# W_out's sums nearer to their loads in three phases, low parts at other places, last halves in tiles of their own

## The chip, the cores and the metric

The kernel runs on one core of one Trainium2 chip. The metric is the device time of one execution in microseconds. The engines are named as in the profile: PE is TensorE, DVE is VectorE, ACT is ScalarE, POOL is GpSimd, SP is SyncE, which here issues nearly all DMAs.

## What is computed

Three stages in a row, all in fp32:

```
# 1. retention: B=2, H=8, S=768, D=64
state = gamma[h] * state + k[:, :, t] (x) v[:, :, t]
y[:, :, t] = scale * q[:, :, t] @ state
# 2. mixture of 8 experts on x [1536, 512], F = 1024
P = exp(x @ w_gate - max); 8 times: P /= rows, P /= columns, P *= N / E
out = sum over e of P[:, e:e+1] * (relu(x @ w1[e]) @ w2[e])
# 3. dense layer, d_ff = 2048
h = x @ w_in;  g = max(h, 0) + alpha * min(h, 0);  y = g @ w_out
```

## The kernel before

**Arithmetic.** An fp32 matmul is done as three fp32r matmuls (mm3, L323 to L325): each operand is split into a high part (a copy rounded to fp32r, made by ACT) and a low part (operand minus high part, made by DVE or POOL), and the products high by high, low by high and high by low are summed in PSUM. So each matrix needs a "high" and a "low" step before PE can use it. Products of 2x2 blocks are done with seven multiplications instead of eight, on sums of the blocks, which are prepared ahead ("sums", "adds").

**Phases.** After the retention part come 20 phases: phase 0 to 7 and 8 to 15 are the eight experts for the two halves of the tokens, 16 to 19 the dense layer as two more "experts" of 1024 columns. Phases 8 to 19 use the seven products for the second layer as well; a phase there has 56 positions: 28 products of the first layer, written (column, product) in the texts, and 28 of the second, written by a number, where the number 1 comes at position 29, 2 at 30 and so on. One position is six matmuls of 128x384 and takes about 1.04 us. While an expert's second phase runs (8 to 15), the kernel also prepares W_out for the dense layer and stores it in DRAM (tensor c).

**Order.** The order is written by hand. `step(ph, pos, fn)` hangs a piece of work behind the PE work of one position; pieces at one position are issued in the order in which they were registered. Each engine carries out its instructions in the order of the program, and so does SP with its DMA issues. What waits, waits with everything behind it on its engine. An entry `[2, ...]` in `unkept` (L302 and others) is issued two positions after the one that appended it.

**What the change touches.** `dense_prep(i)` (L271 and after) prepares one piece of W_out in six steps: `load` (L280, a DMA into the tile dr), `high(0)` (L285, ACT, dw<-dr) whose result is stored two positions later by L310 and L311 (SP), `low(0)` (L289, DVE, into the same tile dw, from dr and dw) stored in the same way, `sums` (L299, four operations of POOL on dr in place), `high(1)`, `low(1)`. Their positions were 6, 14, 24, 27, 40, 52 in each of phases 8 to 15. In a fast phase the hidden layer's blocks b11, b12, b21, b22 come from the first layer's products (copies L977, L997 on ACT, additions L992 on DVE); t1 to t4 (L1059 to L1065, DVE) are their sums, `hhigh` (L1085, ACT) and `hlow` (L1093, DVE) split them into the tiles hs for the second layer. `decode_at` (L882 to L903 on DVE, L892 on ACT) decodes a part of the dense layer's weights between. L179 is the low part of a w1 matrix, L146 its sums, L228 the low part of a w2 matrix, L939 the low part of hidden values in phases 0 to 7. The first loads come from `load_qk` (L471), the last output tiles are written by `last_sum` (L1145 to L1148): one half copied from PSUM by DVE, the other by ACT, each stored by its own DMA queue.

Of the kernel before, what the change touches and what calls it, by code (L numbers as in the profile page):

```python
# [8 lines left out]
F32 = mybir.dt.float32  # L9
# [3 lines left out]
AF = mybir.ActivationFunctionType  # L13
# [10 lines left out]
E, F = 8, 1024  # L24
# [3 lines left out]
HT = S // 2  # L28
# [19 lines left out]
def tile_kernel(ctx, tc, lead, qkT, kv, ctab, w_gate, w1, w2, w_in, w_out, alpha, out):  # L48
    nc = tc.nc
# [392 lines left out]
    with tc.manual_schedule():  # L442

        with ExitStack() as actx:
# [20 lines left out]
            def load_qk(i):  # L465
                if i >= NST:
                    return
                if i == 0:
                    cut = nt + NP * C
                    for cols in (slice(0, cut), slice(cut, lead.shape[1])):  # L470
                        nc.sync.dma_start(out=head[:, cols], in_=lead[:, cols])  # L471
                    halves = head[:, nt:].rearrange("p (v a b c) -> p v a b c", v=2, a=2, c=C)
                    qk_t[i] = lambda r, a, p: halves[r, p // 2, a, p % 2, :]
                else:
                    t = ld.tile([128, 2, NP, C], F32, tag="qk", name=f"qk{i}")
                    nc.sync.dma_start(out=t.rearrange("p a b c -> p (a b c)"), in_=qkT[i])
                    qk_t[i] = lambda r, a, p, t=t: t[r, a, p, :]
# [22 lines left out]
            dve.memset(ones, 1.0)  # L500
            first = tmp.tile([128, HT], F32, tag="d", bufs=2, name="first")
            nc.scalar.activation(out=first[:, 0:1], in_=ones[:, 0:1], func=AF.Copy)
            load_qk(0)
            load_qk(1)
# [636 lines left out]
        def last_sum(ps, m, h):  # L1141
            o = pools["fast"].tile([128, HT], F32, tag=f"t{m}{h}", name=f"last_{m}{h}")
            c = S * (B - 1) + HT * h
            w = HT // 2
            nc.vector.tensor_copy(o[:, 0:w], ps[:, 0:w])  # L1145
            nc.sync.dma_start(out=out[128 * m:128 * m + 128, c:c + w], in_=o[:, 0:w])
            nc.scalar.activation(out=o[:, w:HT], in_=ps[:, w:HT], func=AF.Copy)
            nc.scalar.dma_start(out=out[128 * m:128 * m + 128, c + w:c + HT], in_=o[:, w:HT])  # L1148

# [145 lines left out]
        for ph in range(len(PHASES)):  # L1295
# [41 lines left out]
            else:  # L1337
# [3 lines left out]
                else:  # L1341
# [5 lines left out]
                    for m, part, hi, lo, eng in (  # L1347
                        (2, "a", 5, 5, pool), (2, "c", 9, 9, pool), (2, "b", 11, 12, dve),
                        (3, "a", 13, 16, dve), (3, "c", 14, 14, pool), (3, "b", 17, 17, pool),
                        (4, "a", 25, 26, dve), (4, "c", 30, 31, dve), (4, "b", 37, 37, dve),  # L1350
                        (5, "a", 34, 34, dve), (5, "c", 34, 34, dve), (5, "b", 37, 37, dve),
# [8 lines left out]
                early = ((4, 6, 7, dve), (9, 12, 13, dve), (15, 16, 20, dve), (22, 25, 26, dve))  # L1360
                first = ((6, 6, 7, dve), (12, 13, 14, dve), (20, 20, 20, pool), (24, 24, 24, pool))
                for j, (hi, l0, l1, eng) in enumerate(early if ph else first):
# [5 lines left out]
            if fast:  # L1368
# [7 lines left out]
                if ph < 2 * E:  # L1376
                    step(ph, 0, lambda ph=ph: weight_load(ph))
                    for pos, fn in zip((6, 14, 24, 27, 40, 52), dense_prep(ph - E)):
                        step(ph, pos, fn)
                o = ph < 2 * E  # L1380
                for pos, fn, jp in (
# [3 lines left out]
                    step(ph, pos, lambda ph=ph, fn=fn, jp=jp: fn(ph, jp))  # L1385
                highs = (11, 23, 19, 30 - o, 25, 33 - o, *((32, 34, 36, 38) if o else (33, 34, 37, 39)), 41, 43, 47, 49)
                lows = (13, 26, 20, 31 - o, 27, 34 - o, *((33, 35, 37, 39) if o else (35, 36, 38, 40)), 42, 44, 48, 50)
                for k in range(14):
# [178 lines left out]
```

## Time and profile before

| what | value |
|---|---|
| median of 3 runs | 1256.41 us (1254.65 to 1256.62) |
| the profiled execution's own time | 1257.15 us |
| its span, first to last instruction | 1255.4 us |
| PE busy | 1247.3 us (99%) |
| DVE, ACT, POOL busy | 1010.4, 649.8, 449.0 us |
| mean DMA rate | 299 GB/s |

The busy time of PE is the sum of its matmuls' times, with ends that are modelled; a gap shorter than the overlap of two matmuls does not show in it. The chain of waits follows the last instruction back to what released it, step by step. A row of a timeline gives the start, the busy time, the engine and the line; in brackets stands how long the engine was idle before and what ended that.

### The profile page before, as it was taken

How to read it: one execution, taken by the hardware profiler on the slowest of the kernel's cores; microseconds unless marked ns; L12 is line 12 of the kernel's file. 1: busy time of each engine (PE TensorE's matmuls, PEld its weight loads, DVE VectorE, ACT ScalarE, POOL GpSimd, SP SyncE). 2: the span in 40 equal slices, each digit the busy share in tenths (PEclk: the TensorE clock that was granted, in tenths of full speed). 3: DMA queues.
4: the chain of work that ended last, by engine and by line, in shares of the span. 5: the costliest groups of instructions: out<-in, count | busy, mean ns of one | idle time of the engine just before them, and what ended most of it. 6: DMA issues, size and time to landing. Idle time of an engine off the chain costs nothing.

```text
span 1255.4 us, 20476 instructions
## 1 busy us (share of the span) xinstructions
PE 1247.3 (99%) x7325; PEld 1186.9 (95%) x7325; DVE 1010.4 (80%) x1548; ACT 649.8 (52%) x1204; POOL 449.0 (36%) x407
## 2 busy tenths in 40 slices
PE   9999999999999999999999999999999999999998
PEld 7888989899999989899999999999999999999998
DVE  6676888888888888878596969687877899887867
ACT  5643645453544444446364553545464657656573
POOL 4732343525252625101033333242413464716100
PEclk9999999999999999999999999999999999999999
DMA  9795999999999999899999889898989987694615
GB/s 353 256 275 168 314 339 361 325 354 329 349 327 354 324 352 330 284 348 346 362 308 351 292 320 325 299 349 298 351 303 327 319 281 224 244 314 160 216 37 184
DMA packets 223126, 375.09 MB, mean 299 GB/s; under 512 B 16560, under 2 KB 136752, under 8 KB 223024
## 3 DMA queue, kind: packets, MB, share of 16 engines
q1 hardware_dynamic: 222736, 373.58, 88.0%
q8 instruction: 58, 0.95, 0.3%
q14 instruction: 44, 0.36, 0.1%
q10 hardware_dynamic: 288, 0.20, 0.0%
HBM read 241.04 MB, written 131.11 MB: 296 GB/s over the span
## 4 chain that ended last, share of the span: by engine, by line
PE 87%; DMA 6%; DVE 5%; issue 1%; ACT 0%; SPq 0%; POOL 0%; DVEq 0%; ACTq 0%
PE B L323 7%; PE B L325 7%; PE B L324 7%; PE o L325 7%; PE o L323 7%; PE o L324 7%; PE A L323 6%; PE A L325 6%; PE A L324 6%; PE D L324 4%; PE E L325 4%; PE E L323 4%; PE E L324 4%; PE D L325 4%; PE D L323 4%; DMA dr<-wd 1%
## 5 line engine op out<-in xcount | busy, mean ns | idle before, releaser
L1085 ACT ACTIVATE hs<-b 128x768 fp32r<-128x768 f32 x168 | 139.0, 842 | 66.9 <-DVE b L1059 23.7
L146 POOL TENSOR_TENSOR raw<-raw 128x256 f32<-128x256 f32 x112 | 111.3, 1004 | 69.7 <-DMA raw<-in_w_dram 33.9
L1093 DVE TENSOR_TENSOR hs<-b,hs 128x768 fp32r<-128x768 f32 x120 | 122.4, 1025 | 15.0 <-ACT hs L1085 14.6
L256 POOL TENSOR_TENSOR pr<-pr 128x256 f32<-128x256 f32 x52 | 50.7, 975 | 188.6 <-DMA pr<-in_w_dram 62.2
L323 PE MATMUL A<-xh,W 128*128 128x384 f32 x320 | 107.3, 335 | 0.0
L325 PE MATMUL A<-xh,W 128*128 128x384 f32 x320 | 107.2, 335 | 0.0
L324 PE MATMUL A<-xl,W 128*128 128x384 f32 x320 | 107.0, 334 | 0.0
L323 PE MATMUL B<-hs,ws 128*128 128x384 f32 x288 | 96.4, 335 | 0.2 <-ACT W L169 0.2
L1152 POOL TENSOR_TENSOR total<-total,t 128x384 f32<-128x384 f32 x56 | 73.1, 1333 | 65.4 <-DVE t L1123 65.4
L325 PE MATMUL B<-hs,ws 128*128 128x384 f32 x288 | 96.3, 334 | 0.0
L324 PE MATMUL B<-hs,ws 128*128 128x384 f32 x288 | 96.2, 334 | 0.0
L169 ACT ACTIVATE W<-raw 128x512 fp32r<-128x512 f32 (+1 forms) x126 | 85.9, 695 | 19.3 <-DVE raw L146 19.3
L396 POOL TENSOR_TENSOR xs<-b,xs 128x384 fp32r<-128x384 f32 x19 | 24.6, 1296 | 185.4 <-ACT xs L392 128.5
L323 PE MATMUL B<-xh,W 128*128 128x384 f32 x268 | 90.5, 338 | 0.0
L179 POOL TENSOR_TENSOR W<-raw,W 128x512 fp32r<-128x512 f32 (+1 forms) x48 | 74.5, 1565 | 43.4 <-PE B L325 18.8
L325 PE MATMUL B<-xh,W 128*128 128x384 f32 x268 | 89.7, 335 | 0.0
L324 PE MATMUL B<-xl,W 128*128 128x384 f32 x268 | 89.6, 334 | 0.0
L992 DVE TENSOR_TENSOR b<-E,b 128x384 f32<-128x384 f32 x48 | 26.6, 555 | 74.7 <-ACT W L169 51.9
L977 ACT ACTIVATE B<-A 128x384 f32<-128x384 f32 x48 | 22.8, 476 | 120.6 <-PE A L325 120.4
L299 POOL TENSOR_TENSOR dr<-dr 128x256 f32<-128x256 f32 x32 | 37.9, 1185 | 130.5 <-DVE dw L289 105.5
L323 PE MATMUL D<-xh,W 128*128 128x384 f32 x236 | 79.0, 335 | 0.0
L325 PE MATMUL D<-xh,W 128*128 128x384 f32 x236 | 79.0, 335 | 0.0
(498 smaller groups left out, 4010.2 us busy)
## 6 DMA issues: line engine op xcount, KB each, us to landing
ws<-c SPq DMA_DIRECT2D x168, 512.0 KB, 5.9
raw<-in_w_dram SPq DMA_DIRECT2D x64, 512.0 KB, 5.6
c<-W SPq DMA_DIRECT2D x64, 384.0 KB, 6.5
W<-c SPq DMA_DIRECT2D x22, 768.0 KB, 7.8
pr<-in_w_dram SPq DMA_DIRECT2D x32, 512.0 KB, 5.8
c<-pw SPq DMA_DIRECT2D x32, 512.0 KB, 7.0
c<-pr SPq DMA_DIRECT2D x32, 512.0 KB, 7.6
raws<-in_w_dram SPq DMA_DIRECT2D x32, 384.0 KB, 6.2
```

What stands on the lines that cost most here:

```text
L146: eng.tensor_tensor(out=out, in0=in0, in1=in1, op=op)
L169: nc.scalar.activation(out=hi, in_=src, func=AF.Copy)
L179: eng.tensor_tensor(out=lo, in0=src, in1=hi.bitcast(F32), op=ALU.subtract)
L256: eng.tensor_tensor(out=out, in0=in0, in1=in1, op=op)
L299: nc.gpsimd.tensor_tensor(out=out, in0=in0, in1=in1, op=op)
L323: nc.tensor.matmul(ps, ah, bh, start=first, stop=False, skip_group_check=True)
L324: nc.tensor.matmul(ps, ah, bl, start=False, stop=False, skip_group_check=True)
L325: nc.tensor.matmul(ps, alo, bh, start=False, stop=last, skip_group_check=True)
L992: nc.vector.tensor_tensor(out=dst, in0=src, in1=dst, op=ALU.add)
L1085: nc.scalar.activation(out=t[:, 0, :], in_=hsource(ph, k), func=func)
L1093: nc.vector.tensor_tensor(out=lo, in0=src, in1=hi.bitcast(F32), op=ALU.subtract)
L1152: eng.tensor_tensor(out=dst, in0=dst, in1=tt[m, h], op=ALU.add)
```

## The change

- `load_qk(0)`: the second of the two DMAs that load `head` is issued by ACT instead of SP, and the call stands ahead of ACT's first instruction.
- `last_sum`: the half that ACT copies gets an SBUF tile of its own, under a tag of another buffer.
- Phase 0: the low parts of w1 matrix 3 part a go from position 16 to 14, of matrix 4 part a from 26 to 30 and part c from 31 to 32; the two low parts of w2 matrix 1 go from 13 and 14 to 17 and 18.
- `dense_prep`: in phases 8 and 15 low(0) goes from 24 to 17 and the sums from 27 to 18; in phase 9 high(0) goes from 14 to 18, low(0) from 24 to 21, the sums from 27 to 22. At one position these pieces are registered ahead of t1 and the hhigh and hlow steps.
- Phases 16 to 19: hhigh 0 goes from 11 to 14, hlow 0 from 13 to 16, hlow 4 from 27 to 32.

```diff
--- before.py
+++ after.py
@@ -467,8 +467,8 @@
                     return
                 if i == 0:
                     cut = nt + NP * C
-                    for cols in (slice(0, cut), slice(cut, lead.shape[1])):
-                        nc.sync.dma_start(out=head[:, cols], in_=lead[:, cols])
+                    for cols, eng in ((slice(0, cut), nc.sync), (slice(cut, lead.shape[1]), nc.scalar)):
+                        eng.dma_start(out=head[:, cols], in_=lead[:, cols])
                     halves = head[:, nt:].rearrange("p (v a b c) -> p v a b c", v=2, a=2, c=C)
                     qk_t[i] = lambda r, a, p: halves[r, p // 2, a, p % 2, :]
                 else:
@@ -499,8 +499,8 @@
             warm(WARM)
             dve.memset(ones, 1.0)
             first = tmp.tile([128, HT], F32, tag="d", bufs=2, name="first")
+            load_qk(0)
             nc.scalar.activation(out=first[:, 0:1], in_=ones[:, 0:1], func=AF.Copy)
-            load_qk(0)
             load_qk(1)
             load_kv(0)
             load_kv(1)
@@ -1144,8 +1144,9 @@
             w = HT // 2
             nc.vector.tensor_copy(o[:, 0:w], ps[:, 0:w])
             nc.sync.dma_start(out=out[128 * m:128 * m + 128, c:c + w], in_=o[:, 0:w])
-            nc.scalar.activation(out=o[:, w:HT], in_=ps[:, w:HT], func=AF.Copy)
-            nc.scalar.dma_start(out=out[128 * m:128 * m + 128, c + w:c + HT], in_=o[:, w:HT])
+            o = pools["fast"].tile([128, HT], F32, tag=f"t{m - 2}0", name=f"end_{m}{h}")
+            nc.scalar.activation(out=o[:, 0:w], in_=ps[:, w:HT], func=AF.Copy)
+            nc.scalar.dma_start(out=out[128 * m:128 * m + 128, c + w:c + HT], in_=o[:, 0:w])
 
         def gather(m, h, eng=nc.gpsimd):
             dst = total[:, S * m + HT * h:S * m + HT * h + HT]
@@ -1346,8 +1347,8 @@
                     step(ph, 10, lambda: w1_adds(3, pool))
                     for m, part, hi, lo, eng in (
                         (2, "a", 5, 5, pool), (2, "c", 9, 9, pool), (2, "b", 11, 12, dve),
-                        (3, "a", 13, 16, dve), (3, "c", 14, 14, pool), (3, "b", 17, 17, pool),
-                        (4, "a", 25, 26, dve), (4, "c", 30, 31, dve), (4, "b", 37, 37, dve),
+                        (3, "a", 13, 14, dve), (3, "c", 14, 14, pool), (3, "b", 17, 17, pool),
+                        (4, "a", 25, 30, dve), (4, "c", 30, 32, dve), (4, "b", 37, 37, dve),
                         (5, "a", 34, 34, dve), (5, "c", 34, 34, dve), (5, "b", 37, 37, dve),
                     ):
                         step(ph, hi, lambda m=m, part=part: w1_high(m, part))
@@ -1358,7 +1359,7 @@
                     w1_at(ph, n + 4, dve, dve, 29, 29, 30, 31, 32, 31, 32)
                     w1_at(ph, n + 5, dve, dve, 33, 33, 34, 35, 36, 35, 36)
                 early = ((4, 6, 7, dve), (9, 12, 13, dve), (15, 16, 20, dve), (22, 25, 26, dve))
-                first = ((6, 6, 7, dve), (12, 13, 14, dve), (20, 20, 20, pool), (24, 24, 24, pool))
+                first = ((6, 6, 7, dve), (12, 17, 18, dve), (20, 20, 20, pool), (24, 24, 24, pool))
                 for j, (hi, l0, l1, eng) in enumerate(early if ph else first):
                     step(ph, hi, lambda m=n + j: w2_high(m))
                     step(ph, l0, lambda m=n + j, eng=eng: w2_low(m, 0, eng))
@@ -1375,7 +1376,12 @@
                         step(ph, (2, 5, 8, 11)[q // 2], lambda m=q // 2, h=q % 2: gather(m, h))
                 if ph < 2 * E:
                     step(ph, 0, lambda ph=ph: weight_load(ph))
-                    for pos, fn in zip((6, 14, 24, 27, 40, 52), dense_prep(ph - E)):
+                    places = (6, 14, 24, 27, 40, 52)
+                    if ph in (E, 2 * E - 1):
+                        places = (6, 14, 17, 18, 40, 52)
+                    elif ph == E + 1:
+                        places = (6, 18, 21, 22, 40, 52)
+                    for pos, fn in zip(places, dense_prep(ph - E)):
                         step(ph, pos, fn)
                 o = ph < 2 * E
                 for pos, fn, jp in (
@@ -1383,8 +1389,8 @@
                     (29 - o, t1, 1), (32 - o, t2, 1), (32 if o else 37, t3, 1),
                 ):
                     step(ph, pos, lambda ph=ph, fn=fn, jp=jp: fn(ph, jp))
-                highs = (11, 23, 19, 30 - o, 25, 33 - o, *((32, 34, 36, 38) if o else (33, 34, 37, 39)), 41, 43, 47, 49)
-                lows = (13, 26, 20, 31 - o, 27, 34 - o, *((33, 35, 37, 39) if o else (35, 36, 38, 40)), 42, 44, 48, 50)
+                highs = (11 if o else 14, 23, 19, 30 - o, 25, 33 - o, *((32, 34, 36, 38) if o else (33, 34, 37, 39)), 41, 43, 47, 49)
+                lows = (13 if o else 16, 26, 20, 31 - o, 27 if o else 32, 34 - o, *((33, 35, 37, 39) if o else (35, 36, 38, 40)), 42, 44, 48, 50)
                 for k in range(14):
                     step(ph, highs[k], lambda ph=ph, k=k: hhigh(ph, k))
                     step(ph, lows[k], lambda ph=ph, k=k: hlow(ph, k))
```

## Rows read from the trace of the kernel before

**Rows 1.** Page, part 1: busy us (share of the span) x instructions.

```profile
span 1255.4 us, 20476 instructions
...
PE 1247.3 (99%) x7325; PEld 1186.9 (95%) x7325; DVE 1010.4 (80%) x1548; ACT 649.8 (52%) x1204; POOL 449.0 (36%) x407
```

**Rows 2.** Page, part 4: the chain that ended last, share of the span by engine.

```profile
PE 87%; DMA 6%; DVE 5%; issue 1%; ACT 0%; SPq 0%; POOL 0%; DVEq 0%; ACTq 0%
```

**Rows 3.** Waits of PE, whole span: total us, times, longest.

```profile
PE sc L534 <- DMA qk<-in_qkT_dram: 1.2, 1, 1.2
...
PE E L323 <- ACT E L977: 0.9, 1, 0.9
...
PE o L325 <- DVE hl L939: 0.7, 1, 0.7
```

**Rows 4.** Timeline of DVE, phase 8: start us, us, engine, line, operation [idle before].

```profile
566.37 0.96 DVE L1059 TENSOR_TENSOR b<-b,b 128x768 f32<-128x768 f32 x1 [2.25 <-ACT b L997]
...
569.56 0.69 DVE L887 SCALAR_TENSOR_TENSOR a<-rd,a 128x512 f32<-128x512 uint32 x1
...
574.68 1.23 DVE L289 TENSOR_TENSOR dw<-dr,dw 128x1024 fp32r<-128x1024 f32 x1 [0.77 <-DMA W<-c]
...
577.98 2.43 DVE L1093 TENSOR_TENSOR hs<-b,hs 128x768 fp32r<-128x768 f32 x2
```

**Rows 5.** Tile dw, 547 to 610 us: durations in ns, starts; time to landing.

```profile
L311 SPq DMA_DIRECT2D c<-dw x2: 319/332/346, 567.7 to 577.1; - x2
...
DMA to landing us min/median/max: 6.9/7.7/8.3
```

**Rows 6.** Timeline of ACT, phase 8.

```profile
571.40 0.71 ACT L892 ACTIVATE ex<-ex,ebias 128x512 uint32<-128x512 uint32 x1
...
572.05 0.47 ACT L977 ACTIVATE E<-B 128x384 f32<-128x384 f32 x1
```

**Rows 7.** Timeline of PE, phase 8.

```profile
572.89 0.33 PE L323 MATMUL E<-xh,pairs 128*128 128x384 f32 x1
...
573.95 0.33 PE L323 MATMUL E<-xh,W 128*128 128x384 f32 x1
...
579.23 0.34 PE L323 MATMUL A<-hs,ws 128*128 128x384 f32 x1
```

**Rows 8.** Timeline of ACT, phase 9.

```profile
625.22 1.06 ACT L285 ACTIVATE dw<-dr 128x1024 fp32r<-128x1024 f32 x1 [2.00 <-DMA dr<-wd]
```

**Rows 9.** Timeline of DVE, phase 9.

```profile
630.63 0.69 DVE L887 SCALAR_TENSOR_TENSOR a<-rd,a 128x512 f32<-128x512 uint32 x1
...
638.18 2.44 DVE L1093 TENSOR_TENSOR hs<-b,hs 128x768 fp32r<-128x768 f32 x2
```

**Rows 10.** Tile dw, 620 to 632 us.

```profile
DMA to landing us min/median/max: 4.0/4.0/4.1
```

**Rows 11.** Timeline of DVE, phase 15.

```profile
977.31 0.96 DVE L1059 TENSOR_TENSOR b<-b,b 128x768 f32<-128x768 f32 x1 [2.26 <-ACT b L997]
...
988.17 2.44 DVE L1093 TENSOR_TENSOR hs<-b,hs 128x768 fp32r<-128x768 f32 x2
```

**Rows 12.** Tile dw, 972 to 990 us.

```profile
L310 SPq DMA_DIRECT2D c<-dw x2: 370/370/371, 976.1 to 986.0; - x2
...
DMA to landing us min/median/max: 2.1/4.2/6.3
```

**Rows 13.** Timeline of DVE, phase 0.

```profile
67.79 1.40 DVE L179 TENSOR_TENSOR W<-raw,W 128x512 fp32r<-128x512 f32 x1
```

**Rows 14.** Timelines of DVE in phase 16 and of ACT in phase 17.

```profile
1052.66 0.96 DVE L1093 TENSOR_TENSOR hs<-b,hs 128x768 fp32r<-128x768 f32 x1 [0.91 <-ACT hs L1085]
...
1090.02 0.84 ACT L1085 ACTIVATE hs<-b 128x768 fp32r<-128x768 f32 x1
```

**Rows 15.** Timeline of DVE, start.

```profile
7.45 0.42 DVE L572 TENSOR_TENSOR k<-kt,head 128x256 f32<-128x256 f32 x1 [0.26 <-ACT k L569]
```

**Rows 16.** Windows: us, busy of PE, PEld, DVE, ACT, POOL (x), PEclk, DMA share, GB/s.

```profile
1254.00:1255.40 1.40, 0.00 (x0) 0.00 (x0) 0.00 (x0) 0.00 (x0) 0.00 (x0) 0.65 0.01 2
```

## The prediction

> **What bounds the kernel now.** I began with the busy times and the chain of waits [rows 1, 2]: TensorE is busy 1247.3 of 1255.4 us and holds 87% of the chain that ended last. Nothing that another engine saves shortens this kernel unless TensorE was waiting for it, so I went on to TensorE's own waits [rows 3]. There are few: 1.2 us for the first loads, 0.9 us for a copy of ScalarE, 0.7 us for a low part of VectorE. With short gaps that this view does not list (0.2 to 0.4 us each, read from the starts of neighbouring matmuls, which are 0.173 us apart where nothing waits) some 4.4 us could go, start aside. Everything that makes TensorE wait anew counts in full, because TensorE has no spare time later. So the question for each move is not what it costs its own engine, but whether the work queued behind it still comes before TensorE needs it. I read the engines' timelines around each moved step for that.
>
> The profiled execution took 1257.15 us (1.75 around the span); the median of the runs shown is 1256.41, 0.74 less. I add the change to the median; against the profile the same sum would give 0.74 more. A difference of 0.2%, 2.5 us, is about what a measurement can tell.
>
> **Phase 8, low(0) from position 24 to 17.** This is the term that decides. low(0) overwrites the tile dw, whose high part two DMAs (L310, L311) are still reading, so it waits until both have landed. Its position in the program does not move them: high(0) stays at 14 and the stores are issued two positions later, at 566.5 and 567.7. They take 6.9 us at the least to land [rows 5], in a stretch where the DMA engines are full; landing is at about 574.6, and the row of low(0) shows it: even at position 24 VectorE sat idle 0.77 us before it, and it started at 574.68 [rows 4]. So low(0) at 17 can't start earlier than now, and the sums behind it don't come earlier either. But VectorE takes its work in order, and low(0) now stands ahead of t1 (L1059), which ran at 566.37. All that VectorE did from there to 573.9, 7.3 us of work, goes behind low(0)'s end at 575.9.
>
> Who waits for that: L887 ran at 569.56, three quarters of a microsecond long. After low(0) come t1 (0.96), one L992 (0.47 to the next start), L179, L882, L884 and L887, together 3.2 us, so L887 ends near 579.1. ScalarE's L892 waits for it (0.71, it was at 571.40), and in ScalarE's queue the copy E<-B stands behind that; it was at 572.05 [rows 6] and comes at 579.8 and ends near 580.3. TensorE needs it for the group that began at 573.95 [rows 7]: 6.3 us late. Before it, the group at 572.89 waits for the L992 of 567.96, which now ends at 577.4: 4.5 us without a matmul. Then hlow1 (the first of the two L1093 at 577.98, one half of 2.43 us, so done at 579.2 just as TensorE took it at 579.23) comes behind low(0)'s 575.9 and the 7.3 us, plus the 3.3 us that lay between low(0) and its end now: 586.5, 7.3 us late. From this comes +7.0 us (bounds: 5.7, if the work after the wait packs without the gaps seen now, and 7.9, if POOL's four sums slow the VectorE work beside them as they do now, two L1093 taking 2.43 instead of 1.9 [rows 4]). SP gets stuck as well: the store of low(0)'s result is issued at its new position and waits for 575.9, with three weight loads behind it that went out from 568.2 to 570.9. They go out some 7 us later, but the queue has run empty by 574.6 and TensorE is late by the same 7 us: nothing more for them.
>
> **Phase 9, high(0) 14 to 18, low(0) 24 to 21.** Removed: ScalarE stood 2.00 us in front of high(0) [rows 8], because the load of dr had not landed, and behind it the copy that TensorE lost 0.9 us for [rows 3], with a slower restart 1.1 us. Four positions of 1.04 us cover the 2.0 us. Added: the stores now go out two positions after 18, near 630, and low(0) stands at 21, ahead of t2. VectorE would reach it at 631.3, after L887 [rows 9]. The stores there took 4.0 us [rows 10]; less, if the stall of phase 8 has drained the queue, down to the 2.1 of phase 15 [rows 12]. So VectorE waits to about 633.3, 2 us, and from 630.6 to hlow1's end at 639.2 (half of the row at 638.18) it had no pause to make that up. Net -1.1 - 0.3 (a gap 18 us later) + 2.0 + 0.1: +0.7 us. Bounds: -1.5 (no wait) and +4 (landing 6.9 us after issue as in phase 8).
>
> **Phase 15, low(0) 24 to 17.** The same move, but here the queue is quick: issued at 976.1 and 976.5, 2.1 us at the least [rows 12], landed at 978.7. VectorE is free from 975.05 (2.26 us of idle stand ahead of t1, which ran at 977.31 [rows 11]); t1 now starts at about 980.0 (978.75 + 1.22), 2.7 us late. What catches that up is the 1.22 us that low(0) took later, and a few short idle stretches (0.67, 0.21), at most 1 us of which are usable. hlow1 ended at 989.4 (the first of two at 988.17), TensorE takes it at 990.2. The sums' 5 us go to 980 to 985, and lie beside more of VectorE's two-input work than before, which costs 0.3 to 0.5 for each 128x768 operation. 2.7 - 1.2 - 0.8 + 1.4 = +2.1 us, less a gap of 0.4 late in the phase that goes because w1's sums start earlier: +1.7. Bounds -0.4 (only that gap) and +3.5 (no catching up, full contention).
>
> **Phase 0.** Four low parts move by 1 to 5 positions. The o group waited 0.7 us for hl [rows 3], and a low of 1.40 us held a matmul 0.24 us [rows 13]. Both lose what stood in front of them on VectorE; but the softmax reductions between them wait for a load that landed at 81.0, and this stays. -0.75 us, bounds 0 and -1.2. A raw load that starts after the moved w2 low part goes out 4 us later; it was just in time, so +3 is the far end in the other direction.
>
> **Phases 16 to 19.** hlow4 leaves the queue ahead of t1, so hhigh3 (which made VectorE wait 0.91 us at 1052.66) comes earlier, and hhigh0 (0.84 us on ScalarE) goes from in front of a copy [rows 14]. TensorE's gaps behind them are 0.42 and 0.30 us: -0.7, bounds 0 and -0.7. What is late next is other low parts with a position or more of margin.
>
> **Start and end.** The head's second half goes out on ScalarE's queue, so SP's later loads are issued 0.43 us earlier; but transfers are busy by then and TensorE waits for a landing (1.2 us, [rows 3]): -0.2, bounds -0.45 and +0.3. At the end a tile of its own is to free ScalarE's half from VectorE's copy. I cost it at 0 (bounds -0.35, the length of one copy, and 0): two readers of one PSUM tile stood in order elsewhere too. The copy k<-kt on VectorE started at 7.45, idle until ScalarE's reading of the same kt was done [rows 15]; the bank remains shared, whatever the output tile. The Trainium skill, "PSUM — Partial Sum Buffer", section "PSUM bank collisions raise a hardware error", says that software has to keep two engines off one bank, reads included. If instead the output tile made the order, this edit would give 0.35 us.
>
> **Sum.** +7.0 + 0.7 + 1.7 - 0.75 - 0.7 - 0.2 + 0 = +7.75 us: 1264.2 us on the median (1264.9 on the profile). All lower bounds together make +1.1, all upper ones +18.7; since they are independent I take the root of the sum of squares of the single distances, 3.4 down and 5.5 up, and of the upper one, which leans on two far ends, 4.8.
>
> **Rivals.**
> 1. *The clock falls in the 4.5 us gap of phase 8.* For: after the last matmul (end 1252.0) the granted clock of the last 1.4 us was 0.65 on the mean [rows 16], so it went to the lower level about 2.4 us after TensorE stopped. Against: one instance, and nothing else ran then. Between the gap's end and hlow1 TensorE has six groups of 1.04 us; at half speed 12.5 us, which reaches 590.1 instead of 586.7: at most +3.4, half of it likely, 1266 to 1267.6. The Trainium skill, "TensorE: Matmul & The Clock Gate", section "What's actually happening", has the throttled level as the default that activity releases; by it the fall is to be expected in such a gap. The row at the end agrees.
> 2. *Not slower: the stores of phase 8 land quickly.* The landing there decides all. If the queue were as quick as in phase 15 (2.2 us), low(0) would end at 571.1, hlow1 at 581.8: +2.6 instead of +7.0, and with phase 9 at -1.5 and 15 at 0 the sum is -0.4, 1256.0. It decides below about 3.5 us from issue to landing. Against: 6.9 to 8.3 us in this stretch [rows 5], and nothing ahead of phase 8 changes its loads.
> 3. *Faster: the low parts do not hold up what follows.* If the queue behind low(0) had the slack, all listed gaps would go: -4.4, about 1252. Against: hlow1 ended at 579.2 for a matmul at 579.23; no slack at all.
> 4. *Phase 9 waits as long as phase 8*: +3.3 on the forecast, 1267.5.
>
> **Chances.** Forecast 0.52, rival 1 0.17, rival 4 0.09, rival 2 0.12 (two thirds of it within 0.2%), rival 3 0.10. That is faster 0.13, same 0.09, slower 0.78. The likeliest case's own range is 1260.8 to 1269.0, with rivals 1 and 4 inside its upper end; the range that I give reaches down to the lower edge of rival 2 as well: 1255.5 to 1269.0. Below it lies rival 3, above it their sums.
>
> **What would show it.** Right: in phase 8 VectorE idle some 8 us in front of low(0) until the store's landing, TensorE with a gap near 4.5 us and its next waits on E<-B and L1093; in phase 15 a wait of near 3.5 us in front of low(0). Wrong: low(0) starting near 567, or t1 running ahead of it; TensorE waits no longer than now; a sum of gaps in phase 8 under 3 us. The clock shows in the granted clock of the slices after the gap.

## The result: 17 us slower, twice what was forecast

The changed kernel takes 1273.7 us (median of 4 runs, 1271.08 to 1275.83), the kernel before 1256.51 us beside it. The ratio is 1.0139, 95% interval 1.0117 to 1.0160. The forecast was slower, 1264.2 us; the time lies above the range.

### The profile page after: what moved, and what is told of

Same layout as the page of the kernel before. It is cut to its first block, busy times and chain, and to the rows that moved or that the text cites. A ratio compares the mean times of both kernels' runs of the same rounds, so it can differ in the third digit from the quotient of the medians.

```text
span 1271.6 us, 20481 instructions
## 1 busy us (share of the span) xinstructions
PE 1251.6 (98%) x7325; PEld 1191.7 (94%) x7325; DVE 1007.5 (79%) x1548; ACT 650.3 (51%) x1204; POOL 448.5 (35%) x407
## 5 line engine op out<-in xcount | busy, mean ns | idle before, releaser
L1093 DVE TENSOR_TENSOR hs<-b,hs 128x768 fp32r<-128x768 f32 x120 | 120.9, 1013 | 11.8 <-ACT hs L1085 11.3
L169 ACT ACTIVATE W<-raw 128x512 fp32r<-128x512 f32 (+1 forms) x126 | 85.9, 695 | 19.3 <-DVE raw L146 19.3
L992 DVE TENSOR_TENSOR b<-E,b 128x384 f32<-128x384 f32 x48 | 26.6, 554 | 72.6 <-ACT W L169 51.8
L323 PE MATMUL E<-xh,W 128*128 128x384 f32 x216 | 73.6, 341 | 8.1 <-DVE b L992 7.9
L323 PE MATMUL D<-xh,W 128*128 128x384 f32 x236 | 79.4, 336 | 0.0
```

What stands on the lines that cost most here:

```text
L169: nc.scalar.activation(out=hi, in_=src, func=AF.Copy)
L323: nc.tensor.matmul(ps, ah, bh, start=first, stop=False, skip_group_check=True)
L992: nc.vector.tensor_tensor(out=dst, in0=src, in1=dst, op=ALU.add)
L1093: nc.vector.tensor_tensor(out=lo, in0=src, in1=hi.bitcast(F32), op=ALU.subtract)
```

## The profile after

First the page of the changed kernel, part 1, and TensorE's waits (total us, times, longest):

```profile
span 1271.6 us, 20481 instructions
...
PE 1251.6 (98%) x7325; PEld 1191.7 (94%) x7325; DVE 1007.5 (79%) x1548; ACT 650.3 (51%) x1204; POOL 448.5 (35%) x407
...
PE E L323 <- DVE b L992: 12.7, 3, 5.9
...
DVE dw L289 <- DMA c<-dw: 17.1, 2, 11.1
```

TensorE is still at work for 98% of the span, and the longer span shows as one new line among its waits: three waits, 12.7 us together, on L992 of VectorE (there is no such line in [rows 3]). The last row, from VectorE's waits, says why VectorE was late: low(0) (L289) stood 17.1 us in two waits on the stores that read its tile.

To see where the 16.2 us of the span lie, I took the first matmul of each phase from the trace; the difference of two is a phase's duration. Phases that are not listed differ by less than 0.1 us.

| | before | after | difference | forecast |
|---|---|---|---|---|
| up to phase 0 | 47.68 | 45.91 | -1.78 | -0.2 |
| phase 0 | 66.38 | 68.22 | +1.84 | -0.75 |
| phase 8 | 58.98 | 66.67 | +7.69 | +7.0 |
| phase 9 | 59.88 | 65.80 | +5.92 | +0.7 |
| phase 15 | 58.89 | 62.21 | +3.32 | +1.7 |
| phases 16 and 17 | 117.43 | 116.71 | -0.72 | -0.7 |
| after the last matmul | 3.4 | 3.4 | 0.0 | 0 |

Phase 8 in the changed kernel, timelines of VectorE, ScalarE and TensorE:

```profile
575.20 1.22 DVE L289 TENSOR_TENSOR dw<-dr,dw 128x1024 fp32r<-128x1024 f32 x1 [11.13 <-DMA c<-dw]
...
576.35 0.95 DVE L1059 TENSOR_TENSOR b<-b,b 128x768 f32<-128x768 f32 x1
...
579.96 1.10 DVE L887 SCALAR_TENSOR_TENSOR a<-rd,a 128x512 f32<-128x512 uint32 x1
...
586.43 1.81 DVE L1093 TENSOR_TENSOR hs<-b,hs 128x768 fp32r<-128x768 f32 x2
...
579.08 0.72 ACT L892 ACTIVATE ex<-ex,ebias 128x512 uint32<-128x512 uint32 x1 [0.53 <-DVE ex L882]
...
579.71 0.47 ACT L977 ACTIVATE E<-B 128x384 f32<-128x384 f32 x1
...
577.82 0.69 PE L323 MATMUL E<-xh,pairs 128*128 128x384 f32 x1 [4.80 <-DVE b L992]
...
587.48 0.34 PE L323 MATMUL A<-hs,ws 128*128 128x384 f32 x1
```

It is the picture of the forecast. VectorE is idle for 11.13 us until the stores have landed; low(0) starts at 575.20, no earlier than the 574.68 of before [rows 4]; t1 runs at 576.35 instead of 566.37, L887 ends at 581.06 (forecast 579.1), the copy E<-B starts at 579.71 (forecast 579.8; it was 572.05 [rows 6]), and TensorE has nothing for 4.80 us. hlow1, the first of the two L1093 at 586.43, is done at 587.4 (forecast 586.5), and the matmul that takes it starts at 587.48.

Phase 9, VectorE and the stores' time to land, then TensorE:

```profile
638.01 0.95 DVE L1093 TENSOR_TENSOR hs<-b,hs 128x768 fp32r<-128x768 f32 x1
...
644.93 1.22 DVE L289 TENSOR_TENSOR dw<-dr,dw 128x1024 fp32r<-128x1024 f32 x1 [5.97 <-DMA c<-dw]
...
DMA to landing us min/median/max: 2.1/4.4/6.7
...
649.81 0.69 PE L323 MATMUL E<-xh,W 128*128 128x384 f32 x1 [5.89 <-DVE b L992]
```

Here the forecast failed. high(0) was on time and ScalarE's wait of [rows 8] is gone. But the stores, issued at 637.7 and 638.1, needed up to 6.7 us (4.0 in [rows 10]), and VectorE stood 5.97 us in front of low(0), with t2 and all else behind it; TensorE 5.89 us.

Phase 15, VectorE and TensorE:

```profile
992.39 1.23 DVE L289 TENSOR_TENSOR dw<-dr,dw 128x1024 fp32r<-128x1024 f32 x1 [3.76 <-ACT W L169]
...
995.30 0.96 DVE L882 TENSOR_SCALAR ex<-rd 128x512 uint32<-128x512 uint32 x1
...
1003.83 0.45 PE L323 MATMUL E<-xh,W 128*128 128x384 f32 x1 [2.04 <-DVE b L992]
```

The stores landed after 2.1 to 2.3 us as they did before [rows 12], and VectorE waited 3.76 us all the same (forecast: near 3.5). The row names ScalarE's L169 as what ended the wait; that copy and the second store's landing both fall on 992.2, and low(0) reads nothing of L169.

The clock, windows of the changed kernel in and after the gap of phase 8, in and after that of phase 9 and after that of phase 15, and last the same place of phase 15 in a kernel with W_out's places alone (below); the figure before the DMA share is the granted clock:

```profile
572.00:578.00 6.00, 1.20 (x7) 0.88 (x7) 2.80 (x4) 0.67 (x1) 1.42 (x2) 0.97 0.25 87
...
578.00:584.00 6.00, 5.88 (x18) 5.37 (x19) 5.92 (x8) 4.13 (x9) 2.35 (x3) 0.50 0.81 269
...
644.00:650.00 6.00, 0.19 (x1) 0.19 (x2) 5.03 (x6) 0.84 (x1) 3.39 (x4) 0.65 0.19 67
...
650.00:653.00 3.00, 3.00 (x11) 3.00 (x12) 3.00 (x5) 0.49 (x1) 1.29 (x1) 0.55 0.87 231
...
1004.00:1007.50 3.50, 3.50 (x13) 3.50 (x14) 3.50 (x5) 0.49 (x1) 3.42 (x3) 0.54 0.97 284
...
1002.40:1009.00 6.60, 6.60 (x37) 6.31 (x37) 5.69 (x6) 1.98 (x4) 5.53 (x5) 1.00 0.96 307
```

TensorE had paused for 4.8, 5.9 and 2.0 us, and each time the clock was at the lower of its levels (0.50, 1.2 of 2.4 GHz) for a while, from about 577.6, 645.8 and 1004.3; the windows with 0.97, 0.65, 0.55 and 0.54 hold time at both levels. The last row shows that a gap of 2.0 us doesn't always bring this: there the same pause was followed by 1.00.

Phase 0: the load of raw data for v3 on SP, ScalarE's high part of it, and last the same high part in the kernel before:

```profile
72.03 0.38 SPq L131 DMA_DIRECT2D raw<-in_w_dram  x1
...
78.83 1.06 ACT L223 ACTIVATE v3h<-raw 128x1024 fp32r<-128x1024 f32 x1 [4.92 <-DMA raw<-in_w_dram]
...
76.96 1.06 ACT L223 ACTIVATE v3h<-raw 128x1024 fp32r<-128x1024 f32 x1 [1.00 <-DMA raw<-in_w_dram]
```

The load goes out when the w2 low part that was moved has freed its buffer, at 72.03 (67.00 before), lands at 78.81 (76.94 before), and ScalarE stands 4.92 us in front of v3's high part with the hidden values' high parts behind it. TensorE's o groups then wait three times, 2.7 us by the starts of neighbouring matmuls.

The end: ScalarE's last copy, into its own tile, still starts after VectorE's, which runs from 1268.21 to 1268.57; the second and third row are the two copies in the kernel before:

```profile
1268.60 0.33 ACT L1148 ACTIVATE end<-B 128x192 f32<-128x192 f32 x1 [0.71 <-DVE last L1145]
...
1252.04 0.36 DVE L1145 COPY last<-B 128x192 f32<-128x192 f32 x1 [0.69 <-PE B L325]
...
1252.43 0.33 ACT L1147 ACTIVATE last<-B 128x192 f32<-128x192 f32 x1 [0.71 <-DVE last L1145]
```

## Experiments

All kernels but b_fill, which is the changed kernel with fillers, are the kernel before with a part of the change or another edit. The table has the duration of the phases that differ in the one profiled execution of each, from the first matmuls as above; "0" is the time up to phase 0, ratios are to the kernel before on the same chip, with their interval.

| kernel | 0 | ph 0 | ph 8 | ph 9 | ph 15 | 16+17 | median | ratio |
|---|---|---|---|---|---|---|---|---|
| before | 47.7 | 66.38 | 58.98 | 59.88 | 58.89 | 117.43 | 1256.51 | 1 |
| after | 45.9 | 68.22 | 66.67 | 65.80 | 62.21 | 116.71 | 1273.70 | 1.0139 (1.0117 to 1.0160) |
| a_wout | 46.7 | 66.14 | 65.90 | 66.24 | 61.28 | 117.43 | 1271.86 | 1.0117 (1.0100 to 1.0134) |
| a_start | 45.8 | 66.50 | 59.84 | 60.14 | 58.91 | 117.41 | 1256.41 | 0.9993 (0.9984 to 1.0003) |
| a_phase0 | 46.4 | 68.24 | 60.10 | 59.88 | 58.91 | 117.59 | 1260.89 | 1.0028 (1.0018 to 1.0039) |
| d_w2 | 45.5 | 71.99 | 60.28 | 60.23 | 58.91 | 116.70 | 1259.61 | 1.0016 (1.0007 to 1.0026) |
| d_own8_w1 | 45.5 | 67.59 | 58.35 | 59.63 | 58.89 | 116.92 | 1255.78 | 0.9989 (0.9980 to 0.9998) |
| a_rest | 45.6 | 65.72 | 59.43 | 60.56 | 58.89 | 116.71 | 1255.43 | 0.9987 (0.9978 to 0.9996) |
| b_8_15 | 46.2 | 66.90 | 66.83 | 60.81 | 61.23 | 117.45 | 1268.12 | 1.0089 (1.0074 to 1.0104) |
| b_8_15_own | 47.4 | 65.89 | 58.35 | 58.45 | 59.15 | 117.39 | 1254.88 | 0.9982 (0.9973 to 0.9991) |
| b_fill | 45.5 | 68.76 | 68.75 | 63.72 | 62.04 | 116.70 | 1270.63 | 1.0113 (1.0097 to 1.0130) |
| e_9high | 45.5 | 66.00 | 60.23 | 59.06 | 58.93 | 116.93 | 1253.76 | 0.9974 (0.9962 to 0.9986) |
| c_46 | 45.4 | 66.81 | 60.02 | 58.74 | 58.88 | 116.71 | 1254.97 | 0.9987 (0.9977 to 0.9996) |
| d_16 | 45.7 | 65.65 | 58.92 | 59.52 | 58.91 | 116.81 | 1254.06 | 0.9973 (0.9962 to 0.9983) |
| d_own8 | 45.4 | 66.09 | 58.35 | 58.84 | 58.91 | 116.71 | 1254.02 | 0.9974 (0.9963 to 0.9985) |
| e_both | 45.3 | 66.36 | 58.35 | 58.71 | 58.89 | 116.74 | 1253.23 | 0.9967 (0.9953 to 0.9980) |

A kernel's phases 0, 2, 8 and 9 vary from run to run even where nothing is changed in them: 65.7 to 66.9 us, 62.0 to 63.1, 58.9 to 60.3 and 59.9 to 60.8. Phases 3 to 7 and 10 to 14 differ by 0.5 us at most, and mostly by less than 0.05. What is said of single phases below is above that spread, or said to be within it.

### Which part carries it

**a_wout**, the places of W_out alone:

```diff
-                    for pos, fn in zip((6, 14, 24, 27, 40, 52), dense_prep(ph - E)):
+                    places = {0: (6, 14, 17, 18, 40, 52), 1: (6, 18, 21, 22, 40, 52), 7: (6, 14, 17, 18, 40, 52)}.get(ph - E, (6, 14, 24, 27, 40, 52))
+                    for pos, fn in zip(places, dense_prep(ph - E)):
```

> The kernel before with W_out's places in 8, 9 and 15 alone. If the three places carry the whole slowdown, phases 8, 9 and 15 are longer by about 7.7, 5.9 and 3.3 us as in the changed kernel, 16.9 together, 1273.3 us. Rival: part of it comes from the other edits (phase 0 changes where the DMA queue stands): then the sum is under 14 us.

Measured 1.0117 (1.0100 to 1.0134), some 15 us; the phases are longer by 6.9, 6.4 and 2.4 us, 15.7 together. The three places carry nearly all of the slowdown. Phase 15 is 0.9 us shorter than in the changed kernel: the same gap of 2.0 us, but no fall of the clock (row above).

**a_start**, the hunks of load_qk and last_sum alone:

> The kernel before with the start (head's second half on ScalarE's queue) and the last tile's split alone. The trace after shows phase 0 beginning 1.78 us earlier (45.91 instead of 47.68), because TensorE's wait for qk at 7.70 is gone, and phase 0 giving 1.85 back. Theory A (the moved low parts of phase 0 gave it back): phase 0 keeps the gain, the last matmul ends 1.5 to 1.8 us earlier than before, 1254.7 us. Rival B (phase 0 is tied to something that does not move with the start, the softmax chain behind the load of dm): the gain is lost in phase 0, 1256.4 us. Both: nothing at the very end, ScalarE's last copy still starts after VectorE's.

0.9993 (0.9984 to 1.0003): within the noise. Phase 0 began at 45.81 and lasted 66.50 us, so what was won at the start stays won, as theory A has it; the run then lost 0.9 us each in phases 2 and 8, where nothing was changed. Over all the kernels of this case phase 0 begins at 46.9 us on the mean without this hunk (five profiles, 46.2 to 47.7) and at 45.6 with it (eleven, 45.3 to 45.9): 1.3 us, of which the profile of before, itself a late one, showed more.

**a_phase0**, the hunk of the low parts in phase 0 alone:

> The kernel before with the moves in phase 0 alone. Theory A: the w2 low part at 18 instead of 14 lets the next raw load go out 4 us later; it lands near 80.6 instead of 76.9, its high part follows, and the o groups wait for v3 and hl: phase 1 begins 1.5 to 2.2 us later, 1258.2 us. Rival B (tied to dm's load): phase 0 ends where it ended before, within 0.3 us, 1256.4 us. My prediction's term was -0.75 us.

1.0028 (1.0018 to 1.0039), phase 0 is 68.24 us, as long as in the changed kernel (68.22): +1.9 us. Theory A; my term had the wrong sign. The median is 4.1 us above that of the kernel before on the same chip, more than phase 0 of the profiled execution explains. That execution (1259.62 us) had a granted clock of 1.000 on the mean; the three longest of the eight had 0.997 to 0.999. A fall of the clock in phase 0, as in d_w2 below, would fit, but no profile of a_phase0 shows one.

**d_w2** and **d_own8_w1** take that hunk apart (the first has start, end and 16 to 19 as well, the second also the own tile in phase 8, told below):

```diff
-                first = ((6, 6, 7, dve), (12, 13, 14, dve), (20, 20, 20, pool), (24, 24, 24, pool))
+                first = ((6, 6, 7, dve), (12, 17, 18, dve), (20, 20, 20, pool), (24, 24, 24, pool))    # d_w2
-                        (3, "a", 13, 16, dve), ... (4, "a", 25, 26, dve), (4, "c", 30, 31, dve)
+                        (3, "a", 13, 14, dve), ... (4, "a", 25, 30, dve), (4, "c", 30, 32, dve)    # d_own8_w1
```

> The kernel before with start, end, phases 16 to 19, and only the moved w2 low parts of phase 0. Theory A: phase 0 is 1.8 to 2.5 us longer than with start, end and 16 to 19 alone (65.7 us), as in the changed kernel: 68.2 us; the gap sits in the o groups behind v3's high part. Rival: it takes both moves together, phase 0 under 66.8 us.

> The same with the three moved w1 low parts of phase 0, and the w2 low parts left where they were. If only the w2 low part costs (it lets the next raw load go), phase 0 is 65.6 to 66.5 us as without it, perhaps 0.2 shorter; if the w1 moves cost too, over 67 us.

d_w2: 1.0016 (1.0007 to 1.0026), phase 0 is 72.0 us instead of 65.7 to 66.5: more than expected. ScalarE again stands in front of v3's high part, and here the clock fell as well. The profiled execution (1262.00 us) is 2.4 us above the median of this kernel, so not every execution pays this in full:

```profile
78.65 1.06 ACT L223 ACTIVATE v3h<-raw 128x1024 fp32r<-128x1024 f32 x1 [4.99 <-DMA raw<-in_w_dram]
...
86.00:90.00 4.00, 4.00 (x10) 3.13 (x10) 1.85 (x9) 1.02 (x2) 0.00 (x0) 0.50 1.04 381
```

d_own8_w1: phase 0 is 67.6 us, over the 67 of "the w1 moves cost too". VectorE and TensorE there:

```profile
63.50 1.23 DVE L179 TENSOR_TENSOR W<-raw,W 128x512 fp32r<-128x512 f32 x1
...
64.65 2.31 DVE L228 TENSOR_TENSOR v1l<-raw,v1h 128x512 fp32r<-128x512 f32 x1
...
66.89 0.55 DVE L1027 TENSOR_TENSOR E<-B,d 128x384 f32<-128x384 f32 x1
...
67.50 0.44 PE L337 MATMUL B<-xh,W 128*128 128x384 f32 x1 [1.85 <-DVE E L1027]
```

The w1 low part now stands at 63.50 ahead of the w2 low parts that kept their place, and L1013 (L1027 in this file), which TensorE needs, comes 1.85 us late. So each half of the hunk costs by itself, the w2 half by a late load and ScalarE's queue, the w1 half by VectorE's queue (0.7 us above the longest phase 0 of the kernels that leave it alone); together the second is avoided and the first remains.

**a_rest**, start, end and phases 16 to 19:

> The kernel before with start, end and the moves of phases 16 to 19. 16 and 17 give 0.7 us as in the changed kernel (and as forecast); with theory A on phase 0 the sum is -2.3 to -2.5 us, 1254.0 us; with rival B -0.7 us, 1255.7 us.

0.9987 (0.9978 to 0.9996), 1.3 us faster, between the two expectations; 16 and 17 are 0.72 us shorter as forecast and as in the changed kernel. The three pieces a_wout, a_phase0 and a_rest make up the whole change. Their medians differ from the kernel before by 15.1, 4.1 and -1.3 us, 17.9 together; the whole change measures 17.2.

### What in the places costs

**b_8_15** and **b_8_15_own**. The first is the places of phases 8 and 15 alone, the second takes away what low(0) waits for: it writes a tile of its own, only the three of four blocks that are stored.

```diff
         def low(q):
+            if q == 0 and i in (0, 7):
+                held["l"] = pools["fast"].tile([128, 2, HT], F32R, tag="xs", bufs=2, name=f"dl{i}")
+                l = held["l"].rearrange("p a b -> p (a b)")
+                for to, o, w in ((0, 0, 256), (256, 512, 512)):
+                    nc.vector.tensor_tensor(out=l[:, to:to + w], in0=held["r"][:, o:o + w],
+                        in1=held["w"][:, o:o + w].bitcast(F32), op=ALU.subtract)
+                return
 ...    # put: the two stores of low(0) read this tile
```

> The kernel before with the places of phases 8 and 15 alone. Theory A (low(0) waits for the landing of the two stores that read its tile, and holds VectorE): phase 8 is 6.9 to 7.7 us longer, phase 15 2.4 to 3.3 us, 1266.5 us. It is the pair of the next kernel.

> The same places, but low(0) of phases 8 and 15 writes a tile of its own (the three blocks that are stored, two instructions of 256 and 512 columns, about 0.25 us shorter together), so that it does not wait for the stores of the high part. Theory A: the waits of 10 us and 3.5 us in front of low(0) are gone, phase 8 within 0.7 us of the kernel before and phase 15 within 1 us (it may gain its 0.4 us gap), 1256.5 us. Rival B (not the wait costs, but low(0) and POOL's sums among the two-input work of VectorE at that place): both stay longer, 8 by 2 us or more, 15 by 1.5 us or more, 1260 us or more. Rival C (the stuck SP queue): as A, since the store of the result is issued at once.

b_8_15: 1.0089 (1.0074 to 1.0104). b_8_15_own: 0.9982 (0.9973 to 0.9991). The same positions, the same number of transfers, and 13 us between the medians; in the profiles phases 8 and 15 differ by 10.6 us, phase 9 by 2.4. VectorE's low(0) in the first (one row), then low(0) (L292), t1, the decoding and hlow1 in the second, and a window of the second with TensorE's busy time:

```profile
575.31 1.23 DVE L289 TENSOR_TENSOR dw<-dr,dw 128x1024 fp32r<-128x1024 f32 x1 [11.34 <-DMA c<-dw]
```

```profile
565.99 1.03 DVE L292 TENSOR_TENSOR dl<-dr,dw 128x256 fp32r<-128x256 f32 x2 [1.09 <-ACT dw L285]
...
567.15 0.96 DVE L1073 TENSOR_TENSOR b<-b,b 128x768 f32<-128x768 f32 x1
...
569.73 0.96 DVE L896 TENSOR_SCALAR ex<-rd 128x512 uint32<-128x512 uint32 x1
...
577.87 1.82 DVE L1107 TENSOR_TENSOR hs<-b,hs 128x768 fp32r<-128x768 f32 x2
...
565.00:575.00 10.00, 10.00 (x59) 10.00 (x59) 8.17 (x12) 7.19 (x16) 3.91 (x4) 1.00 1.06 400
```

With a tile of its own low(0) runs at 565.99, as soon as ScalarE is done with the high part, and TensorE has no gap. Theory A; the rival (POOL's sums beside VectorE's work) is refuted for phase 8: the sums lie there beside the decoding and stretch it (0.96 instead of 0.42 us at 569.73), and phase 8 is 58.35 us, as short as any here. Phase 15 is +0.26 us, whose cause was not taken apart. Rival C, the loads that stand behind low(0)'s store on SP, is not separated by this pair, since without the wait they aren't held up either. The traces bear on it: in phase 8 of the changed kernel, of a_wout and of b_8_15 TensorE waits for no load, and its gap ends with VectorE's L992.

**b_fill**, the changed kernel with matmuls of no use in two of the gaps:

```diff
+                for q in range({1: 90, 7: 36}.get(ph - E, 0)):
+                    step(ph, 27, lambda: nc.tensor.matmul(fills[0][:, HT:512],
+                        filler[:, 0:128], filler[:, 0:128], start=True, stop=True, ...))
```

> The changed kernel whole, with matmuls of no use (128 columns of constants, into columns of a bank that nothing reads) between positions 27 and 28, 90 in phase 9 and 36 in phase 15, to keep TensorE at work in its two gaps. Theory A: the lower clock after the gaps costs little, since hlow1 is ready only 1.2 to 1.3 us ahead of its matmul: phase 9 and 15 shorter by 0.9 to 1.3 us each, 1271.5 us; granted clock 1.00 in both phases. Rival B: every matmul that ran at the lower clock counts in full, 1.6 and 1.9 us, 1270.2 us. Rival C: the clock falls by something other than the gap: nothing changes, or the fillers add to the time.

The fillers share a bank with a running sum, so a part of the second layer's sums in phases 9 and 15 is lost. 1270.63 us, ratio 1.0113 (1.0097 to 1.0130), against 1.0139 of the changed kernel; the intervals overlap. The granted clock in two windows behind the gaps:

```profile
648.00:652.00 4.00, 4.00 (x64) 4.00 (x62) 3.97 (x6) 0.43 (x1) 3.58 (x4) 1.00 0.53 163
...
1006.00:1009.00 3.00, 3.00 (x19) 2.90 (x18) 3.00 (x4) 0.49 (x1) 2.92 (x3) 1.00 0.87 281
```

The clock stayed up. In phase 9 the stretch from position 28 to 31 took 3.23 us instead of 4.55, so the fall had cost 1.3 us there. In phase 15 the stretch from 28 to 35 took 8.03 instead of 8.96, the same as in a_wout, where the clock had not fallen without any filler: 0.9 us. Theory A in size. The whole phase 15 gained only 0.2 us, because position 28 came 0.8 us later in that run, and phase 8, where nothing differs from the changed kernel, lost 2.1 us to loads that came late (1.4 and 0.7 us of TensorE's waits, on ws<-c). So the loads held up on SP can cost something too, in one of the four profiles with that stall; the total tells little.

**e_9high**, high(0) of phase 9 at 18 as in the change, low(0) after the landing, with a_rest's hunks:

```diff
+                    places = {1: (6, 18, 30, 33, 40, 52)}.get(ph - E, (6, 14, 24, 27, 40, 52))
```

> The kernel before with start, end, phases 16 to 19, and in phase 9 high(0) at 18 as in the changed kernel, but low(0) at 30 and the sums at 33, after the landing. Theory A (phase 9 of the changed kernel costs 5.9 us by low(0)'s wait on the stores at 21 alone): no gap between 27 and 28, phase 9 58.5 to 59.5 us. Rival (high(0) at 18, behind which copies of ScalarE stand, costs by itself): phase 9 over 60.5 us.

0.9974 (0.9962 to 0.9986), phase 9 is 59.06 us. VectorE around low(0):

```profile
637.49 0.96 DVE L1059 TENSOR_TENSOR b<-b,b 128x768 f32<-128x768 f32 x1
...
638.36 1.22 DVE L289 TENSOR_TENSOR dw<-dr,dw 128x1024 fp32r<-128x1024 f32 x1
...
639.50 0.95 DVE L1093 TENSOR_TENSOR hs<-b,hs 128x768 fp32r<-128x768 f32 x1
...
L310 SPq DMA_DIRECT2D c<-dw x2: 371/397/423, 629.5 to 640.6; - x2
...
DMA to landing us min/median/max: 5.5/5.7/6.0
```

No idle time in front of it, though the stores of phase 9 took 5.5 to 6.0 us here, the two of the high part (issued at 629.5 and 629.9) 5.6 to 5.8. What phase 9 of the changed kernel cost was the place of low(0), with the sums behind it; the later high(0) costs nothing by itself, but its stores are slower. Most of that doesn't come from the stall of phase 8: this kernel has none (with it they took 6.3 and 6.7 us, in a_wout and the changed kernel), while in b_8_15, with that stall and high(0) left at 14, the same two stores took 4.0 to 4.1 us as in the kernel before [rows 10]. It goes with the later place; why the queue is slower there was not taken apart.

### Towards a faster kernel

All on top of a_rest. **c_46** frees dr earlier (low(1) of phase 8 at 46 instead of 52); **d_16** puts high(0) of phase 9 at 16, behind the copy; **d_own8** is the own tile with places (6, 14, 17, 18, 40, 52) in phase 8 alone; **e_both** is d_own8 and d_16 together.

```diff
+                    places = {0: (6, 14, 24, 27, 40, 46)}.get(ph - E, ...)    # c_46
+                    places = {1: (6, 16, 24, 27, 40, 52)}.get(ph - E, ...)    # d_16
+                    places = {0: (6, 14, 17, 18, 40, 52)}.get(ph - E, ...)    # d_own8, with the tile above for i == 0
+                    places = {0: (6, 14, 17, 18, 40, 52), 1: (6, 16, 24, 27, 40, 52)}.get(ph - E, ...)    # e_both
```

> The kernel before with start, end, phases 16 to 19, and low(1) of phase 8 at 46 instead of 52. The copy E<-B in phase 9 stands behind high(0), which waits for dr; dr's load went out only when phase 8's last store (reading the same tile) had landed, at 617.2. Six positions earlier it should land before ScalarE comes to it. Theory A: the 1.1 us gap at 625.5 goes, and nothing takes its place, 1.1 to 1.4 us faster than the same kernel without it, 1254.1 us. Rival: high(0) on time costs the stores' landing ahead of low(0) at 24: VectorE waits there for up to 2 us and the gain is lost.

c_46: 0.9987 (0.9977 to 0.9996), no better than a_rest. Phase 9 is 58.74 us, its gap is gone as theory A says; but phase 8 has a new one of 0.9 us, not the one that the rival named: low(1) at its new place stands ahead of an hlow. TensorE's waits, and VectorE there:

```profile
PE B L324 <- DVE hs L1093: 0.9, 1, 0.9
...
599.27 1.22 DVE L289 TENSOR_TENSOR dr<-dr,dw 128x1024 fp32r<-128x1024 f32 x1
...
601.47 0.95 DVE L1093 TENSOR_TENSOR hs<-b,hs 128x768 fp32r<-128x768 f32 x1
```

> The kernel before with start, end, phases 16 to 19, and in phase 9 only high(0) at 16 instead of 14, behind the copy E<-B on ScalarE. Theory A (the gap of 1.1 us came from the copy standing behind high(0)'s wait): phase 9 is 58.6 to 58.9 us instead of 59.9; the stores leave some 1.5 us later and still land before VectorE comes to low(0) at 24. Rival: what stands behind high(0) now (the copies of positions 16 and 17) makes TensorE wait instead, phase 9 over 59.5 us.

d_16: 0.9973 (0.9962 to 0.9983). Phase 9 is 59.52 us, over theory A's 58.9 and at the edge of the rival's 59.5: 0.4 us under the kernel before, 1.0 under a_rest. TensorE's wait for the copy is gone from its list; what takes the rest was not taken apart. Phase 8 was at the short end of its spread.

> The kernel before with start, end, phases 16 to 19, and in phase 8 alone low(0) at 17 and the sums at 18 with low(0) in a tile of its own. In the kernel with own tiles in 8 and 15 phases 8 and 9 were 0.6 and 1.4 us shorter than before. Theory A (without the wait on the stores the move is worth what it was meant for): phase 8 near 58.4 us, phase 9 near 58.5 us, 16 and 17 together 0.7 us shorter; 2.5 to 3 us under the kernel before, 1253.7 us. Rival: phases 8 and 9 there were short by chance (they spread from 59.0 to 60.1 and from 59.9 to 60.8 us in kernels that leave them alone): then 1255.4 us.

d_own8: 0.9974 (0.9963 to 0.9985). Phase 8 is 58.35 us as in b_8_15_own, under the spread of kernels that leave it alone, and phase 9 58.84.

> The kernel before with start, end, phases 16 to 19, phase 8 with low(0) at 17 in a tile of its own, and phase 9 with high(0) at 16. The two kernels with one of them were at 0.9974 and 0.9973 of before. If their gains in phases 8 and 9 are the same gap (dr on time in phase 9), the two together are no better than one, 1253.5 to 1254.1 us; if they are different, 1 us less, 1253.0 us.

e_both: 1253.23 us beside 1257.16 for the kernel before, 0.9967 (0.9953 to 0.9980). It is faster than the kernel before and than the changed kernel. Beside d_own8 alone the intervals overlap, so whether the gains are one gap or two stays open.

## Why the forecast was wrong

The direction and the main mechanism (low(0) waits for the stores' landing and holds VectorE) were right, the size was not: +7.75 us forecast, +16.2 in the profiled executions, +17.2 in the medians. Of the 8.5 us that are missing in the profiles 5.2 lie in phase 9, 2.6 in phase 0, 1.6 in phase 15 and 0.7 in phase 8; the start gave 1.6 back.

- **Phase 8, +7.0 forecast, +7.7 measured** (6.9 and 7.8 in a_wout and b_8_15): the landing, E<-B and hlow1 came as written. One link was wrong: L892 waits for L882, not L887 (it started at 579.08, while L887 ended at 581.06, 2 us later than forecast); the slower L882 beside POOL's sums made it come out at the same time. The pair with and without an own tile shows that the wait is the cause.
- **Phase 9, +0.7 forecast, +5.9 measured.** This is the step that failed: "So VectorE waits to about 633.3, 2 us", which rested on "less, if the stall of phase 8 has drained the queue". The stores, issued 60 us after that stall, took 6.7 us to land, against 4.0 before. And their place mattered more than the stall: the landing of [rows 10] was read at the old place of the stores, and at the new one they took 5.6 to 5.8 us without any stall (e_9high). The wait was 5.97 us, the gain of 1.1 us came, and the clock added 1.3 us. That was rival 4, at 0.09 and priced at 4.0 us for the phase, without the clock.
- **Phase 15, +1.7 forecast, +3.3 measured.** The wait was sized right (3.76); 0.9 us of the difference is the clock (without its fall the phase cost 2.3 and 2.4 us, in b_8_15 and a_wout). The other 0.7 I put down to contention and less catching up; no run separates them.
- **The clock, rival 1.** It fell after all three gaps, not only after the one that I priced, and where I priced it (up to 3.4 us in phase 8) it seems to have cost next to nothing: position 30 began at 587.48, 0.1 us after hlow1's end, so at full speed TensorE would have waited. No run took the fall out of phase 8. In 9 and 15 it cost 1.3 and 0.9 us, 2.2 us in all. The rival had the fall some 2.4 us after TensorE stops, from the one case at the end [rows 16]; here it came 4.6, 1.9 and 2.5 us after the last matmul, the third time when TensorE was at work again, so this was no fixed delay.
- **Phase 0, -0.75 forecast, +1.85 measured.** The step that failed was to take the raw load that follows the moved low part as a far end (+3) and the two gaps as the likely case. The load was just in time before; 5 us later it was not.
- **Start, -0.2 forecast, -1.3 on the mean.** The loads did land earlier: "transfers are busy by then" was too strong. TensorE's wait of 1.2 us for qk [rows 3] is not in the list of the changed kernel.
- **End, 0, and phases 16 to 19, -0.7:** as forecast.

What the sum missed as a whole: I treated the terms' errors as independent and took the root of their squares. Phases 8, 9 and 15 have the same cause, so they erred the same way; their upper bounds added (+15.4) are near to what they cost (16.9). In rival 2 the terms add to -0.55, not -0.4; nothing hangs on it.

## To carry to other kernels

Before a step is moved towards its inputs, list what else it must wait for: a write into a tile that a store still reads can't start before that store has landed, wherever it stands, and everything behind it on its engine pays. If the step is to come earlier, give it a tile of its own; here that turned +10.2 us in phases 8 and 15 into -0.4 us. Price a landing by the slowest time that the same stretch has shown, not by the one at the old place: moving the store moves it into another part of the queue.

## What the runs showed of the hardware

The decoding's L882 in phase 8 of the kernel before, with no work of POOL beside it:

```profile
568.77 0.42 DVE L882 TENSOR_SCALAR ex<-rd 128x512 uint32<-128x512 uint32 x1
```

- Operations of VectorE with one SBUF input (L882, L884: 0.42 us) took 0.95 to 0.96 us beside POOL's sums, and L887, with two, 1.10 instead of 0.69 [rows 4] (changed kernel, phases 8 and 15). I had counted contention for operations with two inputs alone. The Trainium skill, "SBUF — State Buffer", section "Who interferes with whom", names tensor_scalar among the forms that can use the port pair shared with GpSimd; these rows agree.
- The same pause of TensorE (2.38 us from start to start) was followed by a granted clock of 0.54 in one run and 1.00 in another.
- ScalarE's copy of half a PSUM tile started 0.03 us after VectorE's copy of the other half ended, with separate output tiles as with one. The Trainium skill, "PSUM — Partial Sum Buffer", section "PSUM bank collisions raise a hardware error", asks for such an order by bank; the trace agrees.
